# The last chunk of a long convolution is loaded, combined and stored in another way, and small products wait longer for a host

## The chip, the cores and the metric

The kernel runs on one core of a Trainium2 chip. What counts is the device time of one execution in microseconds (us). Times "of the profile" are taken from one execution that the hardware profiler recorded; its span runs from the first to the last instruction that it saw.

## What is computed

For 2048 tokens of 576 channels, a normalized input goes through two branches: a long convolution over the tokens, whose 2048-tap kernel is made from exponentials and done as a product of Fourier transforms, and a two-layer network per token (576 to 4608 to 576). The output is the input plus the product of the two.

```python
xn = _layernorm(x, axis=-1)
# branch A (_A_ref): convolution along the tokens
K = 2.0 * jnp.einsum("dn,dnl->dl", C, P).real
y = jnp.fft.irfft(jnp.fft.rfft(u_t, L2) * jnp.fft.rfft(K, L2)[None, :, :], L2)[:, :, :L]
s = y.transpose(0, 2, 1) + xn * D_skip[None, None, :]
# branch B: two layers per token, gelu between them
g = _silu(_B_ref(xn, ...))
return x + s * g
```

## The kernel before

**The network** is the large part of TensorE's work. It runs in 48 slots (`NSLOT`, numbered 0 to 47). A slot takes one group of 384 hidden columns and one half of the tokens (`tb` 0 or 1). Three units of 14 matmuls make the hidden columns (`layer1`, L519), and 72 matmuls (`layer2`, L577) multiply them with the second weights for four blocks of 128 tokens, j = 0 to 3. The matmuls write two pairs of accumulator banks in turn, `mxa` and `mxb`. After each block VectorE adds the bank to `acc` (L585), and only then may the next user of that bank begin. ScalarE applies gelu (L552) and splits off a high part (L555), VectorE makes the low part (L558), and these two are what layer 2 reads. The first half of the run does the tokens of blocks 0 to 7, whose gated result goes to the DRAM tensor `g_s` (L605); the second half does blocks 8 to 15.

**The convolution** is cut into 6 chunks of 96 channels (`CH`, `NCH`). Its matmuls are put between those of the network and write a third pair of banks, `cv`. Thirty-six small products (`kgen`, L881), each out of tables that VectorE and ScalarE make from one load of parameters (`load_par`, `par`, L781), give the taps. For each chunk there follow the first transform (`forward`, L953, twice for the taps and twice for the input), four second steps (`s2`, L991), two inverse steps (`inverse`, L1044) and the last step (`i1`, L1076). ScalarE then copies the result out of its banks, and GpSimd's queue stores it by eight DMAs to the DRAM tensor `s_s` (L1087).

**Riding.** A small product either goes alone into the stream, or rides: `ride` hands its matmuls to a larger convolution step (its host), which issues them right ahead of its own, into unused columns of one of its two banks (`lead`). In the kernel before, a step of the lines `c1` (first transforms and second steps) or the step `i1` may be a host, an inverse step may not. The planner lets a product go alone only where TensorE's planned time is `ALONE` = 3 us past its readiness. `END` = 930 spreads the steps of the chunks over the run.

**The end.** Blocks 0 to 7 have their gate in `g_s`, so what is left is out = u + s * g: `combine_load` fetches three pieces into `row` buffers (four exist) on GpSimd's queue, `combine` multiplies and adds on VectorE (L624, L625) and stores by GpSimd's queue (L628). The first four chunks' columns go block by block (eight sets), the columns of the last two chunks in three sets of 3, 3 and 2 blocks, once the last chunk is stored. Blocks 8 to 15 are done in the last two slots by `finish`, out of `acc`: the convolution's result (`last_s`, all 576 columns, after the last chunk's store) sits in `A2`, the input (`last_x`) in the tables' memory. Tanh or silu go through a `row` buffer, too.

**What sets the order.** A planner (`Order`) runs while the program is traced. It holds a clock for each engine, takes steps from lines by their planned readiness, and pins the order in which it took them: the engines and the DMA queues of SP, ACT and POOL (GpSimd) then run in just that order. A step without an engine is a DMA with a guessed time to its landing.

Of the kernel before, what the change touches and what calls it, by code (L numbers as in the profile page):

```python
# [18 lines left out]
P = 128  # L19
NT = 16  # L20
# [192 lines left out]
def mixer_kernel(ctx, tc, u, log_a_real, a_imag, c_real, c_imag, log_dt, d_skip, w1, b1, w2, b2,  # L213
# [396 lines left out]
    def rows_at(t, b, c0, c1):  # L610
        return [dram(t, (b + 16 * y) * D + c0, [[32 * D, 64], [1, c1 - c0]]) for y in range(2)]

    def combine_load(b, n, c0, c1):
        m = c1 - c0
        r = [sb.tile([P, D], F32, name="row", bufs=NROW)[:, :n * m].rearrange("p (i d) -> p i d", i=n) for _ in range(3)]
        nc.gpsimd.dma_start(r[0], u_s[:, b:b + n, c0:c1])
        nc.gpsimd.dma_start(r[1], s_s[:, b:b + n, c0:c1])
        nc.gpsimd.dma_start(r[2], g_s[b:b + n, :, c0:c1].rearrange("i p d -> p i d"))
        XS[b] = r

    def combine(b, n, c0, c1):

        x, s, g = XS[b]
        nc.vector.tensor_mul(s, s, g)  # L624
        nc.vector.tensor_add(x, x, s)  # L625
        for i in range(n):
            for y, o in enumerate(rows_at(out, b + i, c0, c1)):
                nc.gpsimd.dma_start(o, x[64 * y:64 * y + 64, i])  # L628

    def last_x(k):  # L630

        if k == 0:
            TM.extend(table_memory())
        nc.sync.dma_start(TM[k], u_s[:, 8 + k, :])

    def last_s(k):

        m = A2F[:, k * D:(k + 1) * D]
        nc.sync.dma_start(m, s_s[:, 8 + k, :])
        XS[8 + k] = (TM[k], m)  # L640

    TM = []

    def finish(b, c0, c1, silu, end):
# [10 lines left out]
        def mul():  # L655
            s = XS[b][1][:, c]
# [5 lines left out]
        def mul2():  # L662
            s = XS[b][1][:, c]
# [11 lines left out]
        return st + [step("DVE", dve(n), total)]  # L675
# [237 lines left out]
    def chunk(c):  # L913
# [43 lines left out]
        def x1(i):  # L957
            add("PE", X1, lambda: forward(i, 0, lambda r, f: XC[0][r, f, :, 12 * i:12 * i + 12], "p d b -> p b d"), cv=2)
# [104 lines left out]
        def i1():  # L1063
# [17 lines left out]
            def store(f):  # L1081
# [3 lines left out]
                for e in range(4):  # L1085
# [310 lines left out]
    for k in range(8):  # L1396
        tl["steps"].append(step(None, 4.0, lambda k=k: last_x(k), need=[("kg", NB - 1), ("u", NT - 1)], mark=("x8", k)))
# [3 lines left out]
    def end_line():  # L1401
        for c, c0, c1, sets in ((NCH - 3, 0, CE, [(b, 1) for b in range(8)]), (NCH - 1, CE, D, [(0, 3), (3, 3), (6, 2)])):
            for b, n in sets:
                a = (b, n, c0, c1)
                ml["steps"].append(step(None, 12.0 if b else 17.0, lambda a=a: combine_load(*a), need=[("st", c), ("u", NT - 1)]))
                ml["steps"].append(step("DVE", 2 * dve(n * (c1 - c0)), lambda a=a: combine(*a)))
                ml["steps"].append(step(None, 4.0, lambda: None))


    pace = dict(left=NCH * (2 + 2 + 4), last=0.0, started=False)  # L1410
    END = 930.0
# [195 lines left out]
```

## Time and profile before

| | us |
|---|---|
| three runs, median (lowest to highest) | 1081.18 (1080.9 to 1081.19) |
| the profiled execution's own time | 1080.96 |
| its span | 1079.1 |

TensorE's granted clock over the span is 0.998. In the profile PE is TensorE's matmuls, PEld its weight loads, DVE VectorE, ACT ScalarE, POOL GpSimd, SP the engine that issues most DMAs; SPq and ACTq are their DMA issues. L12 is line 12 of the kernel before. A row of the view in order of time gives the start, the duration, engine, line, operation, output<-inputs, the shapes and, in brackets, how long the engine had been idle and what released it. PE's rows overlap, since matmuls are pipelined: what one costs is read from start to start.

### The profile page before, as it was taken

The numbers are of one execution on the slowest core, as the hardware profiler recorded it, in microseconds if no ns is written. First come the engines' busy times: TensorE is split into PE (matmuls) and PEld (weight loads), VectorE is DVE, ScalarE is ACT, GpSimd is POOL, SyncE is SP. The second block draws the span as 40 slices with busy tenths as digits, with TensorE's granted clock in tenths as the row PEclk, the third lists the DMA queues.
The fourth block names the chain that finished last, engine by engine and source line by source line (L and its number), as shares of the span: only waits on it lengthen the run. The fifth ranks groups of instructions, "written<-read, shape, count | busy, mean of one in ns | idle before, by whom it ended". The sixth has DMA issues, their size and how long they took to land.

```text
span 1079.1 us, 25798 instructions
## 1 busy us (share of the span) xinstructions
PE 1067.0 (99%) x10703; PEld 926.3 (86%) x10703; DVE 954.4 (88%) x1535; ACT 689.0 (64%) x1056; POOL 210.3 (19%) x304
## 2 busy tenths in 40 slices
PE   9999999999999999999999999999999999999996
PEld 7989899888888888888888888888888888888896
DVE  7789878999999989999999999999999999677466
ACT  6656768877659685485865767656865756234433
POOL 5669432111100010000200002000010022210222
PEclk9999999999999999999999999999999999999999
DMA  7885556643224231466312234133331455453164
GB/s 234 234 261 185 142 185 211 196 111 129 65 76 123 36 109 53 119 154 130 98 52 67 86 72 115 27 107 76 73 95 53 122 116 153 124 150 108 35 204 118
DMA packets 138565, 129.62 MB, mean 120 GB/s; under 512 B 88636, under 2 KB 109216, under 8 KB 137424
## 3 DMA queue, kind: packets, MB, share of 16 engines
q1 hardware_dynamic: 121792, 78.31, 27.1%
q0 software_dynamic: 15904, 48.70, 14.7%
q8 instruction: 84, 1.38, 0.5%
q10 hardware_dynamic: 752, 0.97, 0.3%
q14 instruction: 33, 0.27, 0.1%
HBM read 98.50 MB, written 35.19 MB: 124 GB/s over the span
## 4 chain that ended last, share of the span: by engine, by line
PE 93%; DVE 2%; ACT 2%; DMA 1%; issue 1%; POOL 0%; SPq 0%; POOLq 0%; DVEq 0%; ACTq 0%
PE mxb L577 21%; PE mxa L519 20%; PE mxa L577 20%; PE mxb L519 20%; PE cv L991 3%; PE cv L881 3%; PE cv L953 2%; PE cv L1044 2%; PE cv L1076 1%; DMA acc<-in_A_u_dram 0%; ACT A L1053 0%; PE mxa L534 0%; DVE pr L720 0%; DMA par<-par_s 0%; DVE acc L585 0%
## 5 line engine op out<-in xcount | busy, mean ns | idle before, releaser
L577 PE MATMUL mxa<-w2h,hh 128*128 128x288 f32 x573 | 171.0, 298 | 1.0 <-DVE acc L585 1.0
L577 PE MATMUL mxb<-w2h,hh 128*128 128x288 f32 x576 | 171.3, 297 | 0.0
L577 PE MATMUL mxb<-w2h,hl 128*128 128x288 f32 x576 | 170.0, 295 | 0.0
L577 PE MATMUL mxb<-w2l,hh 128*128 128x288 f32 x576 | 169.5, 294 | 0.0
L577 PE MATMUL mxa<-w2h,hl 128*128 128x288 f32 x573 | 169.3, 295 | 0.2 <-DVE hl L558 0.2
L577 PE MATMUL mxa<-w2l,hh 128*128 128x288 f32 x573 | 168.7, 294 | 0.0
L558 DVE TENSOR_TENSOR hl<-h,hh 128x512 fp32r<-128x512 f32 x144 | 99.0, 689 | 71.2 <-ACT hh L555 70.5
L577 PEld LDWEIGHTS mxa<-w2h,hh 128*128 128x128 f32 x573 | 107.6, 188 | 9.4 <-issue 4.2
L577 PEld LDWEIGHTS mxb<-w2h,hh 128*128 128x128 f32 x576 | 108.1, 188 | 8.1 <-issue 4.3
L552 ACT ACTIVATE h<-mxa,b1t 128x512 f32<-128x512 f32 x73 | 50.2, 690 | 99.8 <-PE mxa L519 98.7
L577 PEld LDWEIGHTS mxb<-w2l,hh 128*128 128x128 f32 x576 | 108.1, 188 | 0.7
L577 PEld LDWEIGHTS mxa<-w2l,hh 128*128 128x128 f32 x573 | 107.6, 188 | 0.7
L577 PEld LDWEIGHTS mxb<-w2h,hl 128*128 128x128 f32 x576 | 108.1, 188 | 0.0
L577 PEld LDWEIGHTS mxa<-w2h,hl 128*128 128x128 f32 x573 | 107.5, 188 | 0.6 <-DVE hl L558 0.5
L781 POOL DMA_DIRECT2D par<-par_s x36 | 27.4, 761 | 413.5 <-DVE mg L824 399.7
L552 ACT ACTIVATE h<-mxb,b1t 128x512 f32<-128x512 f32 x71 | 49.0, 690 | 83.7 <-PE mxb L519 78.7
L555 ACT ACTIVATE hh<-h 128x512 fp32r<-128x512 f32 x144 | 90.8, 632 | 4.0
L519 PE MATMUL mxa<-XH,w1h 128*128 128x512 f32 x284 | 79.1, 400 | 0.0
L519 PE MATMUL mxb<-XH,w1h 128*128 128x512 f32 x280 | 78.1, 401 | 0.0
L499 ACT ACTIVATE w2h<-raw 128x576 fp32r<-128x576 f32 x75 | 46.3, 674 | 48.0 <-PE mxa L577 44.7
L519 PE MATMUL mxa<-XL,w1h 128*128 128x512 f32 x284 | 76.2, 390 | 0.0
L519 PE MATMUL mxa<-XH,w1l 128*128 128x512 f32 x284 | 76.0, 389 | 0.0
(237 smaller groups left out, 2487.8 us busy)
## 6 DMA issues: line engine op xcount, KB each, us to landing
raw<-in_B_w_dram SPq DMA_DIRECT2D x75, 288.0 KB, 3.3
raw<-in_B_w_dram SPq DMA_DIRECT2D x100, 192.0 KB, 3.4
par_s<-A POOLq DMA_DIRECT2D x8, 1080.0 KB, 5.3
par<-par_s POOLq DMA_DIRECT2D x36, 240.0 KB, 3.8
f2t<-f2q SPq DMA_DIRECT2D x24, 256.0 KB, 3.8
raw<-in_B_w_dram SPq DMA_DIRECT2D x50, 96.0 KB, 3.6
u_s<-in_A_u_dram POOLq DMA_DIRECT2D x16, 288.0 KB, 4.6
xc<-xn_s SPq DMA_DIRECT2D x48, 96.0 KB, 4.0
```

What stands on the lines that cost most here:

```text
L499: nc.scalar.activation(h, r, AF.Copy)
L519: nc.tensor.matmul(q, a, b, start=j == 0, stop=j == len(ops) - 1)
L552: nc.scalar.activation(t, q, AF.Gelu_apprx_tanh, bias=b1t[:, g * G + i:g * G + i + 1], scale=1.0)
L555: LAST[0] = nc.scalar.activation(hh[:, i], t, AF.Copy)
L558: nc.vector.tensor_sub(hl[:, i], t, hh[:, i].bitcast(F32))
L577: nc.tensor.matmul(q[:, dh, :288], a[:, i, c], b[:, i, d], start=i == 0 and k == 0, stop=i == G - 1 and k == 2)
L781: nc.gpsimd.dma_start(PAR[b].rearrange("p (g i) k -> p g (i k)", g=4), dram(par_s, (b // 6 * CH + b % 6 * 4) * NPAR, [[D * NPAR, P], [24 * ...
L881: nc.tensor.matmul(q[32 * g:32 * g + 32, i // 2, i % 2 * 64:i % 2 * 64 + 64], U[:, ri, 4 * g + i, :], v[:, ri, 4 * g + i, :], start=ri == ...
L953: nc.tensor.matmul(Q1ST[i, x][g // 2][64 * f:64 * f + 64, g % 2].rearrange(order), f1t[r].rearrange("p s k -> p (s k)"), rhs(r, f), start= ...
L991: nc.tensor.matmul(Q[i][32 * q:32 * q + 32, f, 2 * ri:2 * ri + 2], m[r, 4 * i + q, 32 * ri:32 * ri + 32], A2[r, 4 * p + 2 * i + q // 2, :, ...
L1044: nc.tensor.matmul(QI[q // 2][64 * h:64 * h + 64, q % 2, i], MAT["g2t", p + h][r, i, ri], YS[p + h][0][r, i, ri], start=ri == 0, stop=ri == 1,
L1076: nc.tensor.matmul(Q[f][32 * e:32 * e + 32, t], g1t[r], A2[r, k:k + 2, 1].rearrange("p i d r -> p i r d"), start=True, stop=True, skip_gro ...
```

## The change

Four things change. (1) Of blocks 8 to 15 the convolution's result is fetched in two parts: the first five chunks' 480 columns earlier (`first_s`, into the tables' memory), the last 96 columns after the last store (`last_s`); the input takes `A2`'s place and is loaded after the last `i1` (`last_x`). (2) For blocks 0 to 7 the fifth chunk's columns become two sets of four blocks, and the last chunk one set of all eight, whose input and gate are loaded ahead of the store, in buffers of `kt` and `xc`; a set is stored by two DMAs, whatever its blocks. The planned landing times are shorter (8 and 12 us for 12 and 17; 9 us for the last piece). (3) `ALONE` is 7.0 for 3.0, `END` 960 for 930, and every step of `c3`, inverse included, may be a host. (4) The stores of a chunk go out in another order of the four pieces.

```diff
@@ -607,39 +607,52 @@
 
     XS = {}
 
-    def rows_at(t, b, c0, c1):
-        return [dram(t, (b + 16 * y) * D + c0, [[32 * D, 64], [1, c1 - c0]]) for y in range(2)]
-
-    def combine_load(b, n, c0, c1):
+    def rows_at(t, b, c0, c1, n=1):
+        return [dram(t, (b + 16 * y) * D + c0, [[32 * D, 64]] + ([[D, n]] if n > 1 else []) + [[1, c1 - c0]])
+                for y in range(2)]
+
+    def combine_load(b, n, c0, c1, part=None):
         m = c1 - c0
-        r = [sb.tile([P, D], F32, name="row", bufs=NROW)[:, :n * m].rearrange("p (i d) -> p i d", i=n) for _ in range(3)]
-        nc.gpsimd.dma_start(r[0], u_s[:, b:b + n, c0:c1])
-        nc.gpsimd.dma_start(r[1], s_s[:, b:b + n, c0:c1])
-        nc.gpsimd.dma_start(r[2], g_s[b:b + n, :, c0:c1].rearrange("i p d -> p i d"))
-        XS[b] = r
+        if part is None:
+            XS[b] = [sb.tile([P, D], F32, name="row", bufs=NROW)[:, :n * m].rearrange("p (i d) -> p i d", i=n) for _ in range(3)]
+        elif part == 0:
+            kt = [sb.tile([P, 12, 64], F32, name="kt", bufs=2).rearrange("p a b -> p (a b)") for _ in range(2)]
+            xc = sb.tile([P, 2, 32, 24], F32, name="xc", bufs=NXC).rearrange("p a b c -> p (a b c)")
+            XS[b] = [t[:, :n * m].rearrange("p (i d) -> p i d", i=n) for t in (kt[0], xc, kt[1])]
+        x, s, g = XS[b]
+        if part != 1:
+            nc.gpsimd.dma_start(x, u_s[:, b:b + n, c0:c1])
+            nc.gpsimd.dma_start(g, g_s[b:b + n, :, c0:c1].rearrange("i p d -> p i d"))
+        if part != 0:
+            nc.gpsimd.dma_start(s, s_s[:, b:b + n, c0:c1])
 
     def combine(b, n, c0, c1):
 
         x, s, g = XS[b]
         nc.vector.tensor_mul(s, s, g)
         nc.vector.tensor_add(x, x, s)
-        for i in range(n):
-            for y, o in enumerate(rows_at(out, b + i, c0, c1)):
-                nc.gpsimd.dma_start(o, x[64 * y:64 * y + 64, i])
+        for y, o in enumerate(rows_at(out, b, c0, c1, n)):
+            nc.gpsimd.dma_start(o, x[64 * y:64 * y + 64])
+
+    TS = []
+    CL = CH * (NCH - 1)
+
+    def first_s(k):
+
+        if k == 0:
+            TS.extend(table_memory())
+        nc.sync.dma_start(TS[k][:, :CL], s_s[:, 8 + k, :CL])
+
+    def last_s():
+
+        for k in range(8):
+            nc.sync.dma_start(TS[k][:, CL:], s_s[:, 8 + k, CL:])
 
     def last_x(k):
 
-        if k == 0:
-            TM.extend(table_memory())
-        nc.sync.dma_start(TM[k], u_s[:, 8 + k, :])
-
-    def last_s(k):
-
         m = A2F[:, k * D:(k + 1) * D]
-        nc.sync.dma_start(m, s_s[:, 8 + k, :])
-        XS[8 + k] = (TM[k], m)
-
-    TM = []
+        nc.sync.dma_start(m, u_s[:, 8 + k, :])
+        XS[8 + k] = (m, TS[k])
 
     def finish(b, c0, c1, silu, end):
 
@@ -653,14 +666,14 @@
             nc.scalar.activation(T[0], z, AF.Silu if silu else AF.Tanh, scale=1.0 if silu else 0.5)
 
         def mul():
-            s = XS[b][1][:, c]
+            s = TS[b - 8][:, c]
             if silu:
                 nc.vector.scalar_tensor_tensor(s, s, 2.0, T[0], op0=OP.mult, op1=OP.mult)
             else:
                 nc.vector.tensor_mul(s, s, z)
 
         def mul2():
-            s = XS[b][1][:, c]
+            s = TS[b - 8][:, c]
             nc.vector.scalar_tensor_tensor(s, T[0], 1.0, s, op0=OP.add, op1=OP.mult)
 
         def total():
@@ -672,7 +685,7 @@
         st = [step("ACT", act(n), act_z, tbl="silu" if silu else "gelu"), step("DVE", dve(n), mul)]
         if not silu:
             st.append(step("DVE", dve(n), mul2))
-        return st + [step("DVE", dve(n), total)]
+        return st + [step("DVE", dve(n), total, need=[("x8", b - 8)])]
 
 
     def params():
@@ -955,7 +968,8 @@
                                      skip_group_check=True)
 
         def x1(i):
-            add("PE", X1, lambda: forward(i, 0, lambda r, f: XC[0][r, f, :, 12 * i:12 * i + 12], "p d b -> p b d"), cv=2)
+            add("PE", X1, lambda: forward(i, 0, lambda r, f: XC[0][r, f, :, 12 * i:12 * i + 12], "p d b -> p b d"), cv=2,
+                mark=("x1", c) if i else None)
             spread(i, 0)
 
         def k1(i):
@@ -1082,7 +1096,7 @@
                 sc = ys_tile().rearrange("p i a b d -> p i (a b) d") if f else (
                     sb.tile([P, 2, 4 * CH], F32, name="pr").rearrange("p t (i d) -> p t i d", i=4))
                 nc.scalar.activation(sc, Q[f].rearrange("p t i r d -> p t (i r) d"), AF.Copy)
-                for e in range(4):
+                for e in (1, 3, 0, 2):
                     y, h = divmod(e, 2)
                     nc.gpsimd.dma_start(s_s[64 * y + 32 * f:64 * y + 32 * f + 32, 8 * h:8 * h + 8, c * CH:(c + 1) * CH],
                                         sc[32 * e:32 * e + 32].rearrange("p t i d -> p (t i) d"))
@@ -1394,22 +1408,26 @@
         for x, y in zip((c1, c2, c3), chunk(c)):
             x["steps"] += y
     for k in range(8):
-        tl["steps"].append(step(None, 4.0, lambda k=k: last_x(k), need=[("kg", NB - 1), ("u", NT - 1)], mark=("x8", k)))
+        tl["steps"].append(step(None, 3.0, lambda k=k: first_s(k), need=[("kg", NB - 1), ("st", NCH - 2)]))
 
     CE = CH * (NCH - 2)
 
     def end_line():
-        for c, c0, c1, sets in ((NCH - 3, 0, CE, [(b, 1) for b in range(8)]), (NCH - 1, CE, D, [(0, 3), (3, 3), (6, 2)])):
+        for c, c0, c1, sets in ((NCH - 3, 0, CE, [(b, 1) for b in range(8)]), (NCH - 2, CE, CL, [(0, 4), (4, 4)])):
             for b, n in sets:
                 a = (b, n, c0, c1)
-                ml["steps"].append(step(None, 12.0 if b else 17.0, lambda a=a: combine_load(*a), need=[("st", c), ("u", NT - 1)]))
+                ml["steps"].append(step(None, 8.0 if b else 12.0, lambda a=a: combine_load(*a), need=[("st", c), ("u", NT - 1)]))
                 ml["steps"].append(step("DVE", 2 * dve(n * (c1 - c0)), lambda a=a: combine(*a)))
                 ml["steps"].append(step(None, 4.0, lambda: None))
+        a = (0, 8, CL, D)
+        ml["steps"].append(step(None, 1.0, lambda: combine_load(*a, 0), need=[("k1", NCH - 1, 1), ("x1", NCH - 1)]))
+        ml["steps"].append(step(None, 9.0, lambda: combine_load(*a, 1), need=[("st", NCH - 1)]))
+        ml["steps"].append(step("DVE", 2 * dve(8 * CH), lambda: combine(*a)))
 
 
     pace = dict(left=NCH * (2 + 2 + 4), last=0.0, started=False)
-    END = 930.0
-    ALONE = 3.0
+    END = 960.0
+    ALONE = 7.0
 
     def pe_turns(limit=1, any_time=False, all_lines=True):
         for x in (nl, pl, ml) + ((c3, c1, kl) if all_lines else ()):
@@ -1427,7 +1445,7 @@
                     pace["left"] -= 1
                 if x is kl and pace["started"] and kl["steps"][0]["mark"][1] < NB - 1 and od.t["PE"] < h[1] + ALONE:
                     break
-                behind = ride(h[0]) if x is c1 or x is c3 and h[0]["mark"][0] == "i1" else None
+                behind = ride(h[0]) if x in (c1, c3) else None
                 od.run(x)
                 if behind:
                     behind()
@@ -1445,8 +1463,9 @@
     later(mid - 4, G - 1, lambda: x_free(0))
     later(mid - 1, G - 1, lambda: x_free(1))
     later(NSLOT - 10, 4, end_line)
+    sl["steps"].append(step(None, 9.0, last_s, need=[("st", NCH - 1)], mark="s8"))
     for k in range(8):
-        c3["steps"].append(step(None, 7.0 if k == 0 else 3.0, lambda k=k: last_s(k), need=[("st", NCH - 1), ("x8", k)], mark=("s8", k)))
+        c3["steps"].append(step(None, 5.0 if k == 0 else 2.0, lambda k=k: last_x(k), need=[("i1", NCH - 1), ("u", NT - 1)], mark=("x8", k)))
 
     def l2_terms(k):
 
@@ -1535,7 +1554,7 @@
                         b = 8 + 4 * tb + j
                         x = el if slot < NSLOT - 1 else od.line()
                         st = finish(b, dh * 288, (dh + k) * 288, slot == NSLOT - 1, slot == NSLOT - 1 and j > 1)
-                        st[0]["need"] = (done, ("s8", b - 8))
+                        st[0]["need"] = (done, "s8")
                         x["steps"] += st
                     elif slot in GATE:
                         for d in range(2):
```

Lines of the kernel after are higher by 13 to 16 in the parts named here (L881 is L894 there, L991 L1005, L781 L794, L1087 L1101, L624 and L625 are L632 and L633).

What the planner makes of it, at three places. **TensorE, slot 28, in layer 2** (XL, XH, w: the network; `cv<-v,U` a small product, `cv<-A` a second step). Before, the product stands alone, and a second step follows 18 matmuls later:

```order
L577 MATMUL mxb<-w2h,hh 128x288
L577 MATMUL mxb<-w2l,hh 128x288
L577 MATMUL mxb<-w2h,hl 128x288
L881 MATMUL cv<-v,U 32x64 x32
L577 MATMUL mxa<-w2h,hh 128x288
L577 MATMUL mxa<-w2l,hh 128x288
L577 MATMUL mxa<-w2h,hl 128x288
```

```order
L577 MATMUL mxa<-w2h,hh 128x288
L577 MATMUL mxa<-w2l,hh 128x288
L577 MATMUL mxa<-w2h,hl 128x288
L991 MATMUL cv<-A_81,f2t 32x192 x32
L577 MATMUL mxb<-w2h,hh 128x288
L577 MATMUL mxb<-w2l,hh 128x288
```

After, at the same place of the network, the two stand together:

```order
L577 MATMUL mxb<-w2h,hh 128x288
L577 MATMUL mxb<-w2l,hh 128x288
L577 MATMUL mxb<-w2h,hl 128x288
L894 MATMUL cv<-v,U 32x64 x32
L1005 MATMUL cv<-A_81,f2t 32x192 x32
L577 MATMUL mxa<-w2h,hh 128x288
L577 MATMUL mxa<-w2l,hh 128x288
L577 MATMUL mxa<-w2h,hl 128x288
```

The product now stands right ahead of a host. Counted over the whole order of TensorE, products alone go from 19 to 8 and riding ones from 17 to 28: with a first transform 10 and 10, with a second step 6 and 13, with an inverse step 0 and 2, with `i1` 1 and 3. The places at which the stream of the network is broken by convolution work go from 85 to 74. The last `i1` stands in slot 45 before and in slot 46 after, each behind the first unit of layer 1.

**GpSimd's queue, second chunk's store** (`par` a parameter load, `s_s` the stores, `g_s` the gate's stores; the number behind `par` counts allocations). Before:

```order
L781 DMA par_5885<-par_s_69 128x4x120
L605 DMA g_s_68<-acc_87 128x576 x4
L1087 DMA s_s_64<-pr_6240 32x8x96 x4
L781 DMA par_6246<-par_s_69 128x4x120
L1087 DMA s_s_64<-ys_6248 32x8x96 x4
L781 DMA par_6400<-par_s_69 128x4x120
L781 DMA par_6578<-par_s_69 128x4x120
```

After:

```order
L794 DMA par_5808<-par_s_69 128x4x120
L605 DMA g_s_68<-acc_87 128x576 x4
L794 DMA par_6256<-par_s_69 128x4x120
L1101 DMA s_s_64<-pr_6405 32x8x96 x4
L1101 DMA s_s_64<-ys_6414 32x8x96 x4
L794 DMA par_6436<-par_s_69 128x4x120
L794 DMA par_6699<-par_s_69 128x4x120
```

Before, a parameter load stands between the two halves of the store; after, one stands ahead of the store and the next behind it.

**VectorE, end of the program** (L585 frees a bank, L624 and L625 are a set's product and sum, L658 to L668 and L671 to L681 the steps of `finish`). The last rows before:

```order
L668 TENSOR_TENSOR w<-w,A_81 128x576
L585 TENSOR_TENSOR acc<-mxa,acc 128x288
L658 SCALAR_TENSOR_TENSOR A_81<-A_81,row 128x576
L585 TENSOR_TENSOR acc<-cv,acc 128x288
L624 TENSOR_TENSOR row<-row 128x384
L625 TENSOR_TENSOR row<-row 128x384
L668 TENSOR_TENSOR v<-v,A_81 128x576
L658 SCALAR_TENSOR_TENSOR A_81<-A_81,row 128x288
L668 TENSOR_TENSOR v<-v,A_81 128x288
L658 SCALAR_TENSOR_TENSOR A_81<-A_81,row 128x288
L668 TENSOR_TENSOR v<-v,A_81 128x288
```

The same end after, in which the two rows of the set are gone:

```order
L585 TENSOR_TENSOR acc<-mxb,acc 128x576
L681 TENSOR_TENSOR A_81<-A_81,w 128x576
L585 TENSOR_TENSOR acc<-mxa,acc 128x288
L671 SCALAR_TENSOR_TENSOR v<-v,row 128x576
L585 TENSOR_TENSOR acc<-cv,acc 128x288
L681 TENSOR_TENSOR A_81<-A_81,v 128x576
L671 SCALAR_TENSOR_TENSOR v<-v,row 128x288
L681 TENSOR_TENSOR A_81<-A_81,v 128x288
L671 SCALAR_TENSOR_TENSOR v<-v,row 128x288
L681 TENSOR_TENSOR A_81<-A_81,v 128x288
```

They now stand in slot 46, behind the second block's add and ahead of the third's:

```order
L585 TENSOR_TENSOR acc<-mxa,acc 128x576
L585 TENSOR_TENSOR acc<-mxb,acc 128x576
L632 TENSOR_TENSOR xc<-xc,kt 128x768
L633 TENSOR_TENSOR kt<-kt,xc 128x768
L585 TENSOR_TENSOR acc<-mxa,acc 128x576
L673 TENSOR_TENSOR w<-w,acc 128x576
L677 SCALAR_TENSOR_TENSOR w<-row,w 128x576
L681 TENSOR_TENSOR A_81<-A_81,w 128x576
L585 TENSOR_TENSOR acc<-mxb,acc 128x576
```

## The prediction

> **What bounds the kernel now.** First the page: its head, the busy times, the chain that ended last.
>
> ```profile
> span 1079.1 us, 25798 instructions
> PE 1067.0 (99%) x10703; PEld 926.3 (86%) x10703; DVE 954.4 (88%) x1535; ACT 689.0 (64%) x1056; POOL 210.3 (19%) x304
> ...
> PE 93%; DVE 2%; ACT 2%; DMA 1%; issue 1%; POOL 0%; SPq 0%; POOLq 0%; DVEq 0%; ACTq 0%
> ```
>
> TensorE is busy for 99% of the span and 93% of the chain is its own, so time is won in three places only: less work or fewer breaks in TensorE's stream, the few spots where it stands, and what comes behind its last matmul. The sum below is made against the profiled execution: span 1079.1 us, its own time 1080.96, so 1.9 lie around the span; it stands 0.2 under the median of the three runs, 1081.18.
>
> **Riding instead of going alone.** The view in order of time, TensorE alone, at three places: a product alone, a second step alone, both together.
>
> ```profile
> 722.86 0.29 PE L577 MATMUL mxb<-w2l,hh 128*128 128x288 f32 x1
> 722.99 0.29 PE L577 MATMUL mxb<-w2h,hl 128*128 128x288 f32 x1
> 723.22 1.10 PE L881 MATMUL cv<-v,U 128*32 128x64 f32 x64
> 724.25 0.40 PE L577 MATMUL mxa<-w2h,hh 128*128 128x288 f32 x1
> ...
> 471.80 0.29 PE L577 MATMUL mxa<-w2h,hl 128*128 128x288 f32 x1
> ...
> 473.54 0.40 PE L577 MATMUL mxb<-w2h,hh 128*128 128x288 f32 x1
> ...
> 863.47 0.29 PE L577 MATMUL mxb<-w2h,hl 128*128 128x288 f32 x1
> 863.70 1.10 PE L881 MATMUL cv<-v,U 128*32 128x64 f32 x64
> 864.73 1.59 PE L991 MATMUL cv<-A,f2t 64*32 64x192 f32 x64
> 866.25 0.40 PE L577 MATMUL mxa<-w2h,hh 128*128 128x288 f32 x1
> ```
>
> Starts count, since matmuls overlap. Two neighbours of layer 2 start 0.13 apart (722.86, 722.99). The product alone puts 724.25 - 722.99 - 0.13 = 1.13 between its neighbours, the second step alone 473.54 - 471.80 - 0.13 = 1.61, both together 866.25 - 863.47 - 0.13 = 2.65. A ride saves 1.13 + 1.61 - 2.65 = 0.09: the matmuls stay, one entry into the stream and one way back go. Eleven more products ride (28 for 17), so **-1.0**. No row shows a ride with an inverse step; there are two, and I bound each from 0 (nothing saved) to 0.18 (twice the row), and take 0.09, the nearest row. A product that waits longer holds its tables and so VectorE's next tables; TensorE's rows show no idle time from that now, and the planner reserves the wait, so I take nothing and keep a new stop of VectorE as a rival.
>
> **The stop at 540.** TensorE's longest idle time after its first matmul is here (GpSimd's queue, VectorE, TensorE, in order of time):
>
> ```profile
> 531.72 2.34 POOL L1087 DMA_DIRECT2D s_s<-pr  x4 [7.04 <-ACT pr L1084]
> 534.05 0.78 POOL L781 DMA_DIRECT2D par<-par_s  x1
> ...
> 537.46 1.23 DVE L799 TENSOR_TENSOR w<-par,tv 128x1024 f32<-128x1024 f32 x1 [1.40 <-DMA par<-par_s]
> ...
> 539.82 0.72 DVE L585 TENSOR_TENSOR acc<-mxa,bias 128x576 f32<-128x576 f32 x1
> ...
> 539.34 0.29 PE L577 MATMUL mxb<-w2h,hl 128*128 128x288 f32 x1
> 540.60 0.40 PE L577 MATMUL mxa<-w2h,hh 128*128 128x288 f32 x1 [0.97 <-DVE acc L585]
> ```
>
> GpSimd's queue issues a parameter load between the two halves of a chunk's store, whose first half waited for ScalarE; so the load starts at 534.05 and VectorE stands 1.40 at L799 until it lands. The adds behind L799 come late, and the bank that TensorE wants next is free only at 540.54: it starts at 540.60, 1.26 behind 539.34, of which 0.13 are normal. Lost: **1.13**. VectorE's waits for parameters over the whole run:
>
> ```profile
> DVE w L799 <- DMA par<-par_s: 2.8, 2, 1.4
> ```
>
> Two times 1.4; the other one reached no matmul. After, the load of this place stands ahead of the store and the next one behind both halves, and every later load in the new order stands outside a store, too. So I let this stop go: **-1.1**. What is late next there is nothing that the rows show: TensorE runs on without idle time up to it and behind it. If it stays or moves, its price is 1.1 again.
>
> **The last chunk, one slot later.** The last `i1` moves to slot 46, at the same place in its slot. Its way to a combined result now (TensorE and GpSimd's queue in slot 45):
>
> ```profile
> 1014.23 1.62 PE L1076 MATMUL cv<-A,g1t 64*32 64x384 f32 x32
> ...
> 1017.10 2.36 POOL L1087 DMA_DIRECT2D s_s<-pr  x4 [25.32 <-ACT pr L1084]
> 1020.64 2.31 POOL L1087 DMA_DIRECT2D s_s<-ys  x4 [1.18 <-ACT h L552]
> ...
> 1024.47 0.77 POOL L617 DMA_DIRECT2D row<-s_s  x1 [0.77 <-DMA s_s<-ys]
> ```
>
> From `i1`'s start (1014.23) to the issue of the load that reads the stored chunk (1024.47) pass 10.24. That load reads blocks 0 to 2 and waits for the seventh store; in the new order of stores the last one belongs to blocks 0 to 7, and a store takes 2.31/4 = 0.58 to issue: 10.8. Then the landing, two VectorE operations of 768 elements and the add that frees the third block's bank, which the new order queues behind them. Durations, and where two slots start on the chain:
>
> ```profile
> row<-s_s POOLq DMA_DIRECT2D x2, 288.0 KB, 4.5
> ...
> L1012 DVE TENSOR_TENSOR pr<-cv,kk 128x768 f32<-128x768 f32 x48 | 45.5, 949 | 0.0
> ...
> 1031.99 3.19 PE mxb L519 x14
> ...
> 1051.05 2.06 PE mxa L519 x9
> ```
>
> The load of 288 KB landed after 4.5; the new one has 384 KB, and I take 4.6. VectorE's operation of 128x768 takes 0.95, the add 0.72 (539.82). So the bank is free 10.8 + 4.6 + 2 x 0.95 + 0.72 = 18.0 after `i1`'s start. TensorE asks for it when slot 47 begins. Slot 46 lasts 1051.05 - 1031.99 = 19.06 now; `i1` adds its 1.6, and it starts behind the first unit of 3.19: 19.06 + 1.62 - 3.19 = 17.5 after `i1`'s start. A new wait of **+0.5**, and each microsecond that the load lands later than 14.9 after `i1` is one of TensorE's. Its bounds, from the same tiles' landing times (stores and their readers; then the row buffers), lowest, middle, highest:
>
> ```profile
> DMA to landing us min/median/max: 2.2/2.6/6.8
> ...
> DMA to landing us min/median/max: 1.8/3.4/6.9
> ```
>
> With the shortest landings (2.2 for a store, 1.8 for a load) nothing is waited for; with the longest, the last store, issued at 1020.64 + 3 x 0.58 = 1022.4, lands 6.8 later, 15.0 after `i1`, the load 6.9 after that, and the wait is 15.0 + 6.9 - 14.9 = 7.0.
>
> The Trainium skill, DMA: Bandwidth & Descriptors, section Specifications, asks for transfers of 512 bytes or more for full rate; the new pieces of 96 columns are 384 bytes long, so the rule speaks against this change. The stores of `s_s` have such rows already and land after 2.6 in the middle, which shows no such loss, so the sum stays. The page gives no size; as an estimate, a landing twice as long, 9.2, would make the wait 5.1 and the time 1082.8, which is a case of rival (b).
>
> The other moved loads I cost at nothing. The eight early pieces take the place of eight larger loads on SP's queue, and the input's eight loads stand behind the last pieces: the first of them is needed by `finish` in slot 46, the last two in slot 47's end, some 15 us after the stores of the blocks ahead of them in that queue. If that cover goes, `finish` waits, and with it VectorE's low part for layer 2. VectorE's own work is the same to 0.1: 8 x 192 columns combined in two steps either way.
>
> **The end.** Behind the last matmul, VectorE, ScalarE and GpSimd in order of time, then the drains at the program's end (lowest, middle, highest ns; first and last start):
>
> ```profile
> 1070.61 0.45 DVE L585 TENSOR_TENSOR acc<-cv,acc 128x288 f32<-128x288 f32 x1
> 1070.98 0.55 DVE L624 TENSOR_TENSOR row<-row 128x384 f32<-128x384 f32 x1
> 1071.56 0.56 DVE L625 TENSOR_TENSOR row<-row 128x384 f32<-128x384 f32 x1
> 1072.04 0.75 DVE L668 TENSOR_TENSOR v<-v,A 128x576 f32<-128x576 f32 x1
> ...
> 1073.57 0.45 DVE L658 SCALAR_TENSOR_TENSOR A<-A,row 128x288 f32<-128x288 f32 x1
> ...
> 1071.56 0.44 ACT L653 ACTIVATE row<-acc 128x288 f32<-128x288 f32 x1 [0.39 <-DVE row L624]
> ...
> 1072.42 2.12 POOL L628 DMA_DIRECT2D out_dram<-row  x4 [12.41 <-DVE row L625]
> ...
> L1603 POOLq DRAIN  x3: 46/103/4587, 1073.8 to 1078.9; - x3
> L1603 SPq DRAIN  x3: 7/7/7, 1077.9 to 1078.6; - x3
> ```
>
> L624 and L625, the last set's combination, stand between the add of 1070.61 and L668: 1072.04 - 1070.98 = 1.06 of the path. They go. What is late next: from L668 to the last L658 VectorE takes 1073.57 - 1072.04 = 1.53, so without the pair it would be there at 1070.98 + 1.53 = 1072.5. But in ScalarE's new order the last silu (0.44 for half a block, as in the row) stands behind the issue of a store that waits for L668's counterpart: 1070.98 + 0.75, an issue of some 0.5 (GpSimd's are 2.12/4 = 0.53), and 0.44 make 1072.7. VectorE waits 0.2. Left: **-0.8**. Then the queues: GpSimd's drain starts at 1073.8 and lasts 4.587, to 1078.35, behind the four late stores of L628; SP's last wait is over at 1077.9. After, GpSimd stores its last set from slot 46 on, over 10 us before the end, so SP decides: **-0.4**. Bounds for both: -1.5 if the silu is not late, -0.4 if SP's stores land no earlier than now.
>
> **Sum.** 1079.1 - 1.0 - 1.1 + 0.5 - 0.8 - 0.4 = 1076.3, and 1.9 around it: **1078.2**, 3.0 under the median, 0.28%. About 0.2%, 2.2 us, is what a measurement of this kernel can tell from no change.
>
> **Rivals.** (a) *A stop as at 540 comes elsewhere.* For it: the order of all engines from slot 9 on is new, and loads of the sets are planned at 8 us for 12; against it: two such stops in the run now. One more costs 1.1, two 2.2: 1079.3 to 1080.4, within 0.2% of before. Chance 0.21. (b) *The last load lands late and slot 47 waits for its bank.* The price is one for one from 14.9 after `i1`. For it: the planner counts 9 us from the copy to the landing, and the rows are longer: 15.4 after `i1` is some 12 after the copy (the first store is issued at 1017.10 - 1014.23 = 2.9, behind the first half's copy). Against it: the rows sum to 0.5 only. At a wait of 1.4 to 5.6 the time is 1079.1 to 1083.3, no change; above 5.6 it is **slower** than before by over 0.2%, and with the longest landings, 7.0, the time is 1078.2 + 6.5 = 1084.7. Chance 0.07 and 0.08. (c) *Rides save nothing*, since what the host gains at one end it loses at the other: 1078.2 + 1.0 = 1079.2, no change. Chance 0.07; three rows speak against it.
>
> For (b) the Trainium skill, TensorE: Matmul & The Clock Gate, Part 1, has a rule more: after an idle window of some 3.4 us the array runs at half clock until it has been busy again. The longest idle time here is 0.97 and the clock 0.998, so no run here shows it; by the rule a wait of 7.0 would cost further microseconds.
>
> **How the numbers follow.** My forecast has 0.57, 1076.6 to 1079.0: the rides and the end known to some 0.5 each, the wait from 0 to 1.3. Faster by over 0.2%, that is under 1079.0: 0.57. Within 0.2%: 0.21 + 0.07 + 0.07 = 0.35. Slower: 0.08. The range takes the forecast's lower end and goes up through (a) and the first part of (b), 1076.6 to 1081.5, which leaves about 0.16 out above and a little below.
>
> **What would show it.** Right: 74 breaks in TensorE's stream, 28 products in front of a host at about 1.04 each; no idle time of TensorE near 540; VectorE standing until `xc<-s_s` lands in slot 46, and TensorE idle by a few tenths at slot 47's first matmul; no L624 and L625 pair behind the last matmul, and SP's drain, not GpSimd's, last. Wrong: TensorE idle for more than 1 us at slot 47's start, or several new idle rows released by L585 or L558, or a last matmul no earlier than now.

## The result, and the profile after

The changed kernel takes 1075.18 us in the median (1075.0 to 1075.71), the kernel before 1081.04 (1080.6 to 1081.19) measured beside it: a ratio of 0.9947, interval 0.993 to 0.9965. It is 5.9 us faster. The forecast had the sign, but 1078.2 is only half of the way, and the time lies 1.4 below the range. The profiled execution took 1075.02. From its page, the head, the busy times and the shares of the chain that ended last:

```profile
span 1073.2 us, 25794 instructions
PE 1063.7 (99%) x10703; PEld 925.9 (86%) x10703; DVE 954.2 (89%) x1535; ACT 690.8 (64%) x1058; POOL 206.3 (19%) x294
...
PE 98%; DVE 1%; DMA 1%; issue 0%; SPq 0%; ACT 0%; ACTq 0%; DVEq 0%
```

The number of matmuls is the same (10703), and TensorE's share of the chain rose from 93% to 98%. Where TensorE's part of the time ends is the start of its last matmul, in the view in order of time, first before, then after:

```profile
1069.82 0.29 PE L577 MATMUL cv<-w2h,hl 128*128 128x288 f32 x1
```

```profile
1066.02 0.29 PE L577 MATMUL cv<-w2h,hl 128*128 128x288 f32 x1
```

So 3.8 us are gone from TensorE's stream (1.6 were forecast), and 2.1 from what comes behind it (1079.1 - 1069.8 = 9.3 before, 1073.2 - 1066.0 = 7.2 after; 1.2 were forecast).

**A break costs more than its first interval.** The forecast measured a product that goes alone from 722.99 to 724.25, the start of the first matmul behind it. The rows that follow in the trace of before:

```profile
724.25 0.40 PE L577 MATMUL mxa<-w2h,hh 128*128 128x288 f32 x1
724.48 0.29 PE L577 MATMUL mxa<-w2l,hh 128*128 128x288 f32 x1
724.62 0.29 PE L577 MATMUL mxa<-w2h,hl 128*128 128x288 f32 x1
```

The next start comes 0.23 later, not 0.13; only from 724.48 on is the spacing normal. All 85 breaks of before and all 74 of after have this second interval, 0.10 to 0.11 too long, in layer 1 and in layer 2. What makes it is not shown. A ride takes one break out of the stream, so it saves 0.09 + 0.105, about 0.20.

**The wait in slot 47 did not come.** After, `i1` (TensorE), GpSimd's queue and VectorE in slot 46, then the last matmul of slot 46 and the first of slot 47:

```profile
1029.55 1.61 PE L1090 MATMUL cv<-A,g1t 64*32 64x384 f32 x32
```

```profile
1032.44 2.31 POOL L1101 DMA_DIRECT2D s_s<-pr  x4 [41.34 <-ACT pr L1098]
1034.74 2.30 POOL L1101 DMA_DIRECT2D s_s<-ys  x4
1039.51 0.89 POOL L627 DMA_DIRECT2D xc<-s_s  x1 [2.46 <-issue]
```

```profile
1043.94 0.96 DVE L632 TENSOR_TENSOR xc<-xc,kt 128x768 f32<-128x768 f32 x1 [0.65 <-DMA xc<-s_s]
1044.93 0.96 DVE L633 TENSOR_TENSOR kt<-kt,xc 128x768 f32<-128x768 f32 x1
1045.81 0.75 DVE L585 TENSOR_TENSOR acc<-mxa,acc 128x576 f32<-128x576 f32 x1
```

```profile
1046.96 0.29 PE L577 MATMUL mxb<-w2h,hl 128*128 128x288 f32 x1
1047.09 1.09 PE L519 MATMUL mxa<-XH,w1h 128*128 128x512 f32 x4
```

VectorE does stand until the load lands, as forecast, but that is at 1043.94, 14.4 after `i1`, and not 15.4. The load was issued 1039.51 - 1029.55 = 9.96 after `i1` (10.8 in the sum): the row of before, from which the sum took its start, held 1.18 of waiting between the two halves of the store, which the changed kernel does not have. VectorE starts 1043.94 - 1039.51 = 4.43 behind the issue (4.6 in the sum; the view of DMAs has 4.3 to the landing). The bank is free at 1045.81 + 0.75 = 1046.56, 0.5 ahead of slot 47, which starts 0.13 behind its neighbour.

**The end.** VectorE's last operations and the drains after (count, lowest, middle and highest ns, first and last start):

```profile
1068.96 0.46 DVE L671 SCALAR_TENSOR_TENSOR v<-v,row 128x288 f32<-128x288 f32 x1 [0.23 <-ACT row L666]
1069.46 0.46 DVE L681 TENSOR_TENSOR A<-A,v 128x288 f32<-128x288 f32 x1
```

```profile
L1622 SPq DRAIN  x3: 7/7/7, 1072.4 to 1072.7; - x3
...
L1622 POOLq DRAIN  x2: 46/74/103, 1072.7 to 1073.0; - x2
```

The last add starts 1069.46 - 1066.02 = 3.44 behind the last matmul, for 1074.06 - 1069.82 = 4.24: 0.8 less, as forecast, with the 0.23 of waiting for the late silu. But from there to the end it is 3.8, for 5.1 before: 1.3 less, where the forecast had 0.4. The landing times of the last stores show why (the view of DMAs from 1060 on, KB each, us from issue to landing), first before, then after:

```profile
out_dram<-row POOLq DMA_DIRECT2D x4, 48.0 KB, 2.6
...
out_dram<-v SPq DMA_DIRECT2D x2, 72.0 KB, 3.1
out_dram<-v ACTq DMA_DIRECT2D x2, 72.0 KB, 3.3
```

```profile
out_dram<-A SPq DMA_DIRECT2D x2, 72.0 KB, 2.2
out_dram<-A ACTq DMA_DIRECT2D x2, 72.0 KB, 2.4
```

GpSimd's four stores are gone from the end, and the same 72 KB of SP and ACT land 0.9 sooner. The forecast let SP decide at its old time.

### The profile page after: what moved, and what is told of

Its sections match the earlier page's. It is cut to its first block, busy times and chain, and to the rows that moved or that the text cites. A ratio compares the mean times of both kernels' runs of the same rounds, so it can differ in the third digit from the quotient of the medians.

```text
span 1073.2 us, 25794 instructions
## 1 busy us (share of the span) xinstructions
PE 1063.7 (99%) x10703; PEld 925.9 (86%) x10703; DVE 954.2 (89%) x1535; ACT 690.8 (64%) x1058; POOL 206.3 (19%) x294
## 3 DMA queue, kind: packets, MB, share of 16 engines
q8 instruction: 84, 1.38, 0.5%
## 4 chain that ended last, share of the span: by engine, by line
PE 98%; DVE 1%; DMA 1%; issue 0%; SPq 0%; ACT 0%; ACTq 0%; DVEq 0%
PE mxa L577 21%; PE mxa L519 21%; PE mxb L577 21%; PE mxb L519 21%; PE cv L894 3%; PE cv L1005 3%; PE cv L966 2%; PE cv L1058 2%; PE cv L1090 1%; DMA acc<-in_A_u_dram 1%; PE mxa L534 0%; PE mxb L534 0%; PE mxa L538 0%; DVE st L372 0%; PE cv L421 0%
## 5 line engine op out<-in xcount | busy, mean ns | idle before, releaser
L577 PE MATMUL mxb<-w2h,hh 128*128 128x288 f32 x576 | 171.0, 297 | 0.0
L577 PE MATMUL mxa<-w2h,hh 128*128 128x288 f32 x573 | 170.3, 297 | 0.0
L577 PE MATMUL mxb<-w2h,hl 128*128 128x288 f32 x576 | 170.1, 295 | 0.0
L577 PE MATMUL mxa<-w2h,hl 128*128 128x288 f32 x573 | 169.5, 296 | 0.1
L577 PE MATMUL mxb<-w2l,hh 128*128 128x288 f32 x576 | 169.5, 294 | 0.0
L577 PE MATMUL mxa<-w2l,hh 128*128 128x288 f32 x573 | 168.6, 294 | 0.0
L794 POOL DMA_DIRECT2D par<-par_s x36 | 27.4, 762 | 463.6 <-DVE mg L837 411.9
L577 PEld LDWEIGHTS mxb<-w2h,hh 128*128 128x128 f32 x576 | 108.1, 188 | 6.9 <-issue 3.0
L577 PEld LDWEIGHTS mxa<-w2h,hh 128*128 128x128 f32 x573 | 107.6, 188 | 7.4 <-issue 5.3
L577 PEld LDWEIGHTS mxb<-w2l,hh 128*128 128x128 f32 x576 | 108.2, 188 | 0.7
L577 PEld LDWEIGHTS mxb<-w2h,hl 128*128 128x128 f32 x576 | 108.1, 188 | 0.1
L577 PEld LDWEIGHTS mxa<-w2l,hh 128*128 128x128 f32 x573 | 107.6, 188 | 0.7
L577 PEld LDWEIGHTS mxa<-w2h,hl 128*128 128x128 f32 x573 | 107.5, 188 | 0.6 <-DVE hl L558 0.5
L585 DVE TENSOR_TENSOR acc<-mxa,acc 128x576 f32<-128x576 f32 x88 | 65.5, 744 | 12.0 <-PE mxa L577 11.9
```

The costliest lines, as they stand in the source:

```text
L577: nc.tensor.matmul(q[:, dh, :288], a[:, i, c], b[:, i, d], start=i == 0 and k == 0, stop=i == G - 1 and k == 2)
L585: nc.vector.tensor_add(o, q[:, dh:dh + n, :288], b if first else o)
L794: nc.gpsimd.dma_start(PAR[b].rearrange("p (g i) k -> p g (i k)", g=4), dram(par_s, (b // 6 * CH + b % 6 * 4) * NPAR, [[D * NPAR, P], [24 * ...
```

## The experiments: rides and the two halves of the change

Theory A is the price of 0.20 for a ride, theory B the 0.09 of the forecast. The two halves are the riding (part 3 of the change) and the end (parts 1, 2 and 4).

**The new end without the new riding.** In the changed kernel:

```diff
-    END = 960.0
-    ALONE = 7.0
+    END = 930.0
+    ALONE = 3.0
-                behind = ride(h[0]) if x in (c1, c3) else None
+                behind = ride(h[0]) if x is c1 or x is c3 and h[0]["mark"][0] == "i1" else None
```

> The changed kernel with the old riding rule, ALONE 3 and END 930: parts 1, 2 and 4 of the change alone. TensorE has the 85 breaks of before. Theory A (a break costs 0.10 more than was counted, in the interval behind the first matmul that follows it, so a ride saves 0.20): span 1073.2 + 11 x 0.20 + 1.3 for the stop of VectorE, which is back because a parameter load stands between two stores again = 1076.7. Theory B (a ride saves 0.09 as counted, the rest of the gain lies in the end or in the order): 1073.2 + 1.0 + 1.3 = 1075.5. Behind the last matmul both expect 7.2 as in the changed kernel.

Measured: span 1077.1, ratio to before 0.9984 (0.9975 to 0.9993). The last matmul starts at 1069.86, as before, and 7.2 stand behind it. The stop near 540 is back; after it, TensorE's rows:

```profile
539.17 0.29 PE L577 MATMUL mxb<-w2h,hl 128*128 128x288 f32 x1
540.68 0.40 PE L577 MATMUL mxa<-w2h,hh 128*128 128x288 f32 x1 [1.22 <-DVE acc L585]
```

It costs 540.68 - 539.17 - 0.13 = 1.38. Take it off, and 1077.1 - 1073.2 - 1.4 = 2.5 are left for eleven breaks, 0.23 each. Programs with the same order on TensorE differ by up to 1.8 in when slot 46 starts, so one difference of two profiles is not exact; but all eleven executions span 1076.2 to 1077.5, over B's 1075.5, and summed over the breaks themselves (both intervals) this run has 2.1 more than the changed kernel, 0.20 a break: A. The new end alone is worth the 2.1 behind the last matmul.

**The new riding without the new end.** In the kernel before:

```diff
-    END = 930.0
-    ALONE = 3.0
+    END = 960.0
+    ALONE = 7.0
-                behind = ride(h[0]) if x is c1 or x is c3 and h[0]["mark"][0] == "i1" else None
+                behind = ride(h[0]) if x in (c1, c3) else None
```

> The kernel before with the new riding rule, ALONE 7 and END 960: part 3 alone. TensorE has the 74 breaks of the changed kernel. Theory A: its last matmul starts 11 x 0.20 + 1.4 = 3.6 earlier than before (1069.8), at 1066.2, and behind it stand 9.3 as before: span 1075.5. Theory B (0.09 a ride): last matmul at 1069.8 - 1.0 - 1.4 = 1067.4, span 1076.7. On the end: if GpSimd's four late stores slow the last stores of SP and ACT, these land 3.1 to 3.3 after their issue as before, not 2.2 to 2.4.

Measured: 1089.42, ratio 1.0084 (1.0071 to 1.0098), slower than before; span 1087.6. The stream is as A has it: the last matmul starts at 1066.78, with 0.89 of waiting at slot 47, without which it would be 1065.9. But 20.8 stand behind it, which neither theory expected. (SP's and ACT's last stores land in 2.1 to 2.4, not the 3.1 to 3.3 of before: GpSimd's stores come later than these here.) VectorE and GpSimd's queue there:

```profile
1070.65 0.75 DVE L624 TENSOR_TENSOR row<-row 128x576 f32<-128x576 f32 x1
1071.43 0.76 DVE L625 TENSOR_TENSOR row<-row 128x576 f32<-128x576 f32 x1
1080.31 0.56 DVE L624 TENSOR_TENSOR row<-row 128x384 f32<-128x384 f32 x1 [8.12 <-DMA row<-g_s]
```

```profile
1072.49 3.16 POOL L628 DMA_DIRECT2D out_dram<-row  x6 [11.56 <-DVE row L625]
1075.64 0.73 POOL L616 DMA_DIRECT2D row<-u_s  x1
```

The third set's loads stand behind the second set's stores, and these behind VectorE. With the last `i1` in slot 46, the old end with its three sets, one behind the other, no longer fits under the network. So the two halves are not worth a sum: the end alone brings 2.0 of span, the riding alone costs 8.5, both together bring 5.9. The riding half makes the last `i1` late, and the rebuilt end takes that up. Which part of the half does it, `ALONE`, `END` or the rule for hosts, was not tried one by one; that it need not be a ride, the next run shows, where nothing rides and, with `END` = 960, `i1` stands in slot 46 all the same.

**No rides at all.** In the changed kernel:

```diff
-    ALONE = 7.0
+    ALONE = 0.0
-                behind = ride(h[0]) if x in (c1, c3) else None
+                behind = None
```

> The changed kernel in which no product rides: 36 go alone, 102 breaks for 74. Theory A: 28 x 0.20 = 5.6 more, and 1.3 for the stop of VectorE (a parameter load stands between two stores again): span 1080.1. Theory B: 28 x 0.09 = 2.5 and 1.3: 1077.0.

Measured: span 1080.4, ratio to before 1.0018 (1.0008 to 1.0028). A's total holds, but by luck: one of its terms was wrong, and another of the same size was missing. There is no stop near 540 (the parameter load does stand between the stores there, at 534.01, and no matmul is late). In its place slot 47 waits for its bank, VectorE first, then TensorE:

```profile
1051.40 0.96 DVE L632 TENSOR_TENSOR xc<-xc,kt 128x768 f32<-128x768 f32 x1 [2.54 <-DMA xc<-s_s]
```

```profile
1052.53 0.29 PE L577 MATMUL mxb<-w2h,hl 128*128 128x288 f32 x1
1054.08 1.20 PE L519 MATMUL mxa<-XH,w1h 128*128 128x512 f32 x4 [1.26 <-DVE acc L585]
```

`i1` starts at 1035.12 here, so the load landed 16.3 behind it, 1.4 past the 14.9 of the forecast, and TensorE lost 1054.08 - 1052.53 - 0.13 = 1.42. The last matmul starts at 1073.12, 7.1 later than in the changed kernel; without 1.4 that is 5.7 for 28 breaks, 0.20 each (5.4, 0.19 each, summed over the breaks themselves).

**Waiting still longer for a host.** In the changed kernel `ALONE = 12.0`:

> The changed kernel with ALONE 12: 72 breaks for 74, so TensorE's stream is 0.4 shorter, but the last step i1 stands in slot 47, not 46. By the way from i1 to the landing (14.4 to 15) the last chunk is there some 17 us into slot 47 of 19, and the steps of finish for eight blocks, 3 us of VectorE each block, come behind it: span 1083 or more. Rival (the steps of finish are still hidden): 1072.8.

Measured: span 1082.4, ratio 1.0028 (1.0015 to 1.0042). The last `i1` starts at 1045.37, 1.5 ahead of slot 47's first matmul. The last matmul is in place (1065.92), but VectorE first gets to `finish` at 1058.72 and then runs without a pause to its last add:

```profile
1058.72 0.75 DVE L673 TENSOR_TENSOR w<-w,acc 128x576 f32<-128x576 f32 x1
```

```profile
1077.65 0.46 DVE L681 TENSOR_TENSOR A<-A,v 128x288 f32<-128x288 f32 x1
```

That is 11.7 behind the last matmul, for 3.4. An `i1` that is later by most of a slot costs 9.2 of span, more than the whole change had won.

## The experiments: the load and the end

**The load of the last combination, four copies later**, and ten (`range(10)`):

```diff
+        if part == 1:
+            for k in range(4):
+                nc.gpsimd.dma_start(g_s[0, k:k + 1, :8], s_s[:1, 7, c0:c0 + 8])
         if part != 0:
             nc.gpsimd.dma_start(s, s_s[:, b:b + n, c0:c1])
```

> The changed kernel with four tiny copies from the stored chunk to DRAM in GpSimd's queue ahead of the last combination's load; they wait for the same stores and, at 0.6 to 0.8 us to issue, push the load by 2.4 to 3.2. In the changed kernel the load lands 14.4 after the last step i1, 0.5 ahead of the 14.9 from which the forecast has TensorE wait in slot 47. If that mechanism holds, slot 47's first matmul is 1.9 to 2.7 late and the span 1075.1 to 1075.9, one for one. Rival (the bank's release is not what slot 47 needs first): no wait, span 1073.2.

> The same with ten copies, 6 to 8 us of issue: a wait of 5.5 to 7.5, span 1078.7 to 1080.7 if it is one for one. By the Trainium skill, TensorE: Matmul & The Clock Gate, Part 1, an idle window of some 3.4 us halves TensorE's clock until it has been busy again for about as long; then the units behind the wait are longer than 3.2 each and the span grows by 1.7 or more beyond the wait, and the granted clock falls in that stretch.

With four, nothing happened: ratio 0.9953 (0.9937 to 0.9969), and slot 47 starts on time (the span, 1074.1, is 0.9 longer, but so late is slot 46 already, at 1027.13 for 1026.26, ahead of the copies). GpSimd's queue:

```profile
1037.88 2.07 POOL L628 DMA_DIRECT2D g_s<-s_s  x4
1040.29 0.91 POOL L630 DMA_DIRECT2D xc<-s_s  x1 [0.33 <-issue]
```

The copies went out right behind the last store's issue and filled the 2.5 that the load had waited anyway, so it was issued 9.9 after `i1` (1030.42 to 1040.29) as without them. The expectation had added them to the wait.

With ten copies the time is 1081.19 (1079.0 to 1082.87), ratio 1.0 (0.9989 to 1.001); the profile is of the longest of eight executions. The load landed at 1048.90, 18.1 after `i1` (1030.81), 3.2 past the bound. GpSimd's queue and VectorE, TensorE's rows, and its clock in three stretches (busy, matmuls, granted clock, DMA share, GB/s):

```profile
1038.30 5.06 POOL L628 DMA_DIRECT2D g_s<-s_s  x10
1048.90 0.96 DVE L635 TENSOR_TENSOR xc<-xc,kt 128x768 f32<-128x768 f32 x1 [4.28 <-DMA xc<-s_s]
```

```profile
1048.28 0.29 PE L577 MATMUL mxb<-w2h,hl 128*128 128x288 f32 x1
1051.57 2.08 PE L519 MATMUL mxa<-XH,w1h 128*128 128x512 f32 x4 [3.00 <-DVE acc L585]
...
1057.29 0.63 PE L519 MATMUL mxa<-XR,w1s 128*128 128x512 f32 x1
1057.71 0.67 PE L519 MATMUL mxb<-XH,w1h 128*128 128x512 f32 x2
```

```profile
1053.00:1056.00 3.00, 3.00 (x8) 0.50 0.69 160
1056.00:1058.00 2.00, 2.00 (x7) 0.55 0.76 191
1058.00:1060.00 2.00, 2.00 (x10) 1.00 0.90 195
```

The wait is 1051.57 - 1048.28 - 0.13 = 3.16: one for one with the landing. Then the unit takes 1057.71 - 1051.57 = 6.14 at half clock, 2.95 more than the 3.19 of a unit. The span, 1080.8, is 7.6 longer than the changed kernel's: 6.1 from here, and 1.3 already when slot 46 starts (1027.53 for 1026.26), where the two programs have the same order; the rest, 0.2, is not explained. The wait is about half of the 5.5 to 7.5 that were expected, again because the copies fill waiting first; that the span comes out near 1080.7 is luck, since the slow clock and the late start make up for it.

**Four more stores at the end.** In `total` of the changed kernel, when `end` is set and b is 14:

```diff
+                for y in range(2):
+                    for i in range(2):
+                        nc.gpsimd.dma_start(g_s[4 * y + 2 * i:4 * y + 2 * i + 2, :64, CL:].rearrange("i p d -> p i d"),
+                                            x[64 * y:64 * y + 64, 192 * i:192 * i + 192].rearrange("p (i d) -> p i d", i=2))
```

> The changed kernel with four stores of 48 KB more on GpSimd's queue behind the second last add (to a DRAM tensor that nothing reads any more), as the kernel before had them there. If these stores are what made the last stores of SP and ACT land late, these land 3.1 to 3.3 after their issue for 2.2 to 2.4 now, GpSimd's drain ends last, and 8.5 to 9 us lie between the last matmul's start and the end of the span, for 7.2. Rival (the stores of before landed late because of what their own queues did): GpSimd's drain alone may end late, the landing stays at 2.2 to 2.4.

Measured: 1077.51, ratio 0.9972 (0.9961 to 0.9982); its eight executions span 1075.0 to 1077.5, the changed kernel's four 1073.1 to 1073.9. The profile is of the shortest, span 1075.0, with the last matmul (1065.97) and the last add (1069.41) where the changed kernel has them. The landing times from 1060 on, and the drains:

```profile
out_dram<-A SPq DMA_DIRECT2D x2, 72.0 KB, 3.1
out_dram<-A ACTq DMA_DIRECT2D x2, 72.0 KB, 3.2
```

```profile
L1627 POOLq DRAIN  x3: 46/103/4839, 1069.4 to 1074.7; - x3
L1627 SPq DRAIN  x3: 7/7/7, 1073.5 to 1074.5; - x3
```

Both effects of the kernel before are back: SP's and ACT's stores land 0.9 later (SP's drain starts at 1073.5, not 1072.4), and GpSimd's drain outlasts them, 1069.4 + 4.8 = 1074.2. Behind the last matmul stand 9.0. The rival is out.

**The last silu freed of an issue.** One of ACT's three stores (block 14's second half) on SP's queue, then on GpSimd's:

```diff
-                        st = finish(b, ..., slot == NSLOT - 1 and j > 1)
+                        st = finish(b, ..., slot == NSLOT - 1 and j > 2)
```

```diff
-                queue = nc.scalar if end and y else nc.sync
+                queue = (nc.gpsimd if b == 14 else nc.scalar) if end and y else nc.sync
```

> The changed kernel with one of ACT's three late stores (block 14's second half) on SP's queue, so that the last silu does not stand behind its issue. If that issue holds the end, as the forecast has it (0.2), VectorE's last add starts 0.2 to 0.3 earlier, and the span is 0.2 shorter, 1073.0. Rival: SP's queue is late with one issue more (0.47 each), and the end stays at 1073.2 or comes 0.2 later.

> The changed kernel with one of ACT's three late stores (block 14's second half) on GpSimd's queue, which has nothing else to do there. VectorE's last add starts 0.3 earlier against the last matmul (3.1 behind it for 3.4), as in the run with that store on SP, and SP has no issue more. GpSimd's drain ends some 3.7 behind its last issue (1074.22 - 1070.50 in the run with four stores more), here at about 1071.9 on the changed kernel's time axis, ahead of SP's 1072.4: span 0.3 shorter, 72.9 in place of 73.2. Rival: one store on GpSimd's queue is enough to make the others land 0.5 to 0.9 later, and the span is 0.2 to 0.6 longer.

In both the silu is no longer late: the last add starts 3.1 behind the last matmul (1068.73 - 1065.62, and 1070.36 - 1067.23), for 3.4. It brings nothing that can be measured: ratios 0.9952 (0.994 to 0.9965) and 0.9948 (0.9934 to 0.9962), the changed kernel's 0.9947. On SP the 0.3 is eaten and 0.2 more, as the rival had it: 7.4 stand behind the last matmul (1073.0 - 1065.6), and the span of 1073.0 comes only from a last matmul that is 0.4 earlier. On GpSimd 7.0 stand behind it (1074.2 - 1067.2) and its last matmul is 1.2 later; GpSimd's drain (4.0 from 1069.4) ends a little behind SP's (1073.2), not ahead of it. The other stores land no later than in the changed kernel (2.2 to 2.3). No version beat the changed kernel clearly.

**The old order of a chunk's stores**, `for e in range(4)`:

> The changed kernel with the old order of the stores of a chunk, part 4 undone alone. The last combination's load then waits for the seventh store and not the eighth, is issued 0.6 earlier and lands 13.8 after i1 for 14.4; the eight small loads of last_s wait for the eighth store, not the seventh, and land 0.6 later. TensorE waits for neither (the bound is 14.9), so the time is the same, span 1073.2 within 0.3. Rival: last_s comes late for finish in slot 46 and VectorE is late for slot 47: 0.5 more.

Ratio 0.9949 (0.9936 to 0.9962): no difference, as expected. The load is issued 9.4 after `i1` (1030.07 to 1039.47), 0.6 earlier, but lands 14.3 after it (1044.33), not 13.8, since it took 4.86 for 4.43.

## Why the forecast was half of it

Of the 3.1 that were missed, 1.2 lie in a cost of the rides that the forecast left out, 0.9 in the landing of the last stores, 0.5 in a wait that did not come, and the rest in small differences. The measured figures of the first three rows are sums over all of TensorE's rows, before and after (first intervals 128.5 and 127.4 beyond the normal spacing, second intervals 9.1 and 7.9).

| term | forecast | measured | |
|---|---|---|---|
| rides, first intervals | -1.0 | -1.1 | right |
| rides, second intervals | none | -1.2 | the step that failed |
| stops of TensorE (540 and others) | -1.1 | -1.3 | right |
| wait in slot 47 | +0.5 | 0 | mis-sized, inside its bounds |
| not told apart, in the stream | none | -0.2 | |
| path to the last add | -0.8 | -0.8 | right |
| from the last add to the end | -0.4 | -1.3 | mis-sized |
| span | -2.8 | -5.9 | |

**Rides.** "A ride saves 1.13 + 1.61 - 2.65 = 0.09" is the step that failed. The three measurements end with the start of the first matmul behind the break, and so leave out the second interval, which every break has once, whether one step stands in it or a product and its host. It cancels between a host alone and a host with a product, but not against the product that goes alone: two breaks become one. 11 x 0.105 = 1.2 were missing. The runs with 85 and 102 breaks (0.23 and 0.20 a break, working from whole streams) bear it out. The two rides with an inverse step put 2.61 between their neighbours, 0.09 less than the parts (1.12 + 1.58), as assumed; one of them, after:

```profile
775.72 0.39 PE L519 MATMUL mxa<-XR,w1s 128*128 128x512 f32 x1
776.04 1.10 PE L894 MATMUL cv<-v,U 128*32 128x64 f32 x64
777.07 1.56 PE L1058 MATMUL cv<-ys,g2t 32*64 32x192 f32 x64
778.56 0.73 PE L519 MATMUL mxb<-XH,w1h 128*128 128x512 f32 x2
```

Neighbours of layer 1 start 0.23 apart, so this is 778.56 - 775.72 - 0.23 = 2.61. Rival (c) falls.

**The stop at 540** went as forecast. Counted over TensorE's rows, spacing that was over 0.15 too long without a break came to 1.64 in three places before (1.13 of it at 540) and to 0.36 in two after. The load there stands ahead of the store, and TensorE's list of waits has no L577 behind L585 any more. It belongs to the riding half: the run with the old riding has it, the runs with the new riding do not. A load between the two halves of the store does not make it by itself, as the run without rides shows. Rival (a) did not happen.

**Slot 47.** The mechanism (VectorE stands for the load, the bank behind it, TensorE from 14.9 on, one for one) is shown by two runs, 1.42 for 1.4 and 3.16 for 3.2; the size was off by 0.9 in the issue and 0.2 in the landing, so the changed kernel runs 0.5 clear of it. Rival (b) is what the changed kernel comes near to, not what it does. The load's 384 KB, in pieces of 384 bytes, landed in 4.3, the 288 KB of before, in pieces of 768 bytes, in 4.5. The rule of the Trainium skill (DMA: Bandwidth & Descriptors, Specifications) that the forecast weighed, 512 bytes or more, shows no loss here.

**The end.** The path to the last add was right in each step. "SP decides: -0.4" took SP's landing from a profile in which GpSimd's stores were in flight beside it. For both terms of the end together the bounds were -1.5 to -0.4, the latter "if SP's stores land no earlier than now"; that a store takes less time to land was in neither, and -2.1 came. That four such stores cause it is shown by putting them back. "SP's drain, not GpSimd's, last" came true.

That the two halves need each other was not in the forecast at all: it priced the riding for itself and the later `i1` as a wait, and never asked what the old end would have done with it.

## What to carry to other kernels

When a break in a pipelined stream is priced from start to start, go on until the spacing is normal again; the cost left out is small for one break and the same for every one. Before a landing time is carried over to a changed end, ask what else was in flight beside it. Where a change has two halves, ask what each would do without the other: here one half is worth something only because the other takes up the lateness that it makes.

## What was not expected of the hardware

In the profile with ten copies TensorE's granted clock fell to 0.50 at 1051.0, 2.4 us behind the end of its last matmul (1048.57) and while it still stood idle. It rose again at 1057.8, after 6.2 us of work at half (512 columns every 0.43 for 0.23), so that a wait of 3.2 cost 6.1. Idle times of 1.26 and 1.22 in the other runs left it at full. The eight executions of that program do not agree: their spans go from 1076.8, with a mean granted clock of 0.998 as in the changed kernel, to 1080.8 with 0.996, so the half clock did not last equally long in all of them and may have been missing in the shortest. The Trainium skill, TensorE: Matmul & The Clock Gate, Part 1, gives a window of some 3.4 us for both. In this profile a shorter idle time was enough, and the way back took longer.

Two stores of 72 KB on each of two queues took 3.1 to 3.3 to land with four stores of 48 KB of a third queue beside them, and 2.0 to 2.7 without (2.4 or less in all runs but the one with `ALONE` = 12, where thirteen stores of 144 KB stand on SP's queue from 1060 on, for five in the changed kernel).
